# Retention attention and SwiGLU on one core: a hand-written opening order replaced by steps of the list scheduler

## The chip, the core and the metric

The kernel runs on one core of one Trainium2 chip. A core has a matrix engine (TensorE, PE; its weight loads are shown apart as PEld), three engines for elementwise work (VectorE, DVE; ScalarE, ACT; GpSimd, POOL), and a synchronisation engine (SP) that here issues the loads. Each engine works off its own queue in order; semaphores hold an instruction until what it needs is done. The metric is the device time of the run in microseconds (us).

## The reference

```python
def _attn_ref(q, k, v, lam):               # q, k, v: (4, 8, 768, 64) fp32
    ...
    for b in range(nb):                    # blocks of 64 positions
        intra = np.einsum('bhic,bhjc->bhij', qb, kb) * Dmask[None]
        intra = np.einsum('bhij,bhjd->bhid', intra, vb)
        inter = np.einsum('bhid,bhde->bhie', qb * lam_pow[None], kv_state)
        out[:, :, sl] = intra + inter
        kv_state = lam_block[None, :, None, None] * kv_state + np.einsum('bhsd,bhse->bhde', kb_dec, vb)

def _moe_ref(x, w_gate, w_val, w_out, rms_g):
    rms = np.sqrt(np.mean(x * x, axis=-1, keepdims=True) + 1e-06)
    xn = x / rms * rms_g
    g = xn @ w_gate                        # 512 -> 1536
    silu = g * (1.0 / (1.0 + np.exp(-g)))
    val = xn @ w_val
    return (silu * val @ w_out).astype(np.float32)
```

The output of the attention, 3072 tokens of 512 values, is the `x` of the second part.

## The kernel before, in words

The tokens are six groups `m` of 512. For each group the attention is done for four pairs `p` of heads (`Pair(m, p)`); then the rows are normed (`Norm`), and the group goes through the gated layer in twelve blocks `f` of 128 hidden columns (`Hidden(m, f)`). One such (m, f) is a unit `u`. Units 0 to 5 are group 0 with blocks 0 to 5, units 6 to 17 group 1 with all twelve, units 18 to 23 group 0 with blocks 6 to 11; group 0's rows are kept in `partial` in between. From unit 24 on come groups 2 to 5, in another form of the products (`tx`, `pa`, `pb`).

fp32 products are made of fp16 or f32r high and low parts, three products each (`hl`, `hh` against `wo`; high and low `x` against high and low `wg`, `wv`). For that, each weight block is loaded as integers (`raw_gv`, 1 MB; `raw_o`, 512 KB), lifted to floats by ACT (`lift`, L222), converted by DVE in two steps (`convert`, L231 and L234), squared by ACT for a norm (`square`, L446, output `junk`), summed over partitions on PE (`norm`, output `pn`, L451), scaled (`scale`, outputs `e`, `sc`), and split into a high part by ACT (L469) and a low part by DVE (L473). Later each block gets column sums of squares: ACT squares (`sq_w`, L305), DVE adds (`add`, L311; `last`, L314), and PE sums them (`pc`, L325), between the value matmuls of a unit.

The names of PE's outputs: `pa` scores, `pst` state sums, `po` mixes (attention out), `pss` row sums of squares, `pr` spread norms, `pg` gate, `pv` value, `acc` output product. DVE's `a` is a score tile times the decay mask (L533). `pc` and the second tile of `pa` share the PSUM bank `ps1`. `busy(n)` puts n matmuls of the identity with an unread output into PE's queue (`unread`), fillers in short. `load_next` issues the next load of a fixed list on SP's queue: the pairs `q1_0` to `q1_3` of group 1 between the weight blocks `gv1`, `gv2`, and so on; `load_o(f)` issues block f's output weights. A tile of tag `in` has four buffers, one of `raw_o` two: a load waits, and with it all that is queued behind it on SP, until the tile that had the buffer was read.

What sets the order: from unit 6 on a list scheduler (`Plan`) that knows for each step its engine, a cost in us, a due time `at` in units, the keys it reads (`r`) and writes (`w`) and the buffers it opens (`new`); it keeps a clock for each engine and emits the steps in order of their start. DVE steps in the set `SHARED` and POOL steps are taken to exclude each other. Units 0 to 5, the attention of groups 0 and 1, and weight blocks 0 to 5 are instead put in order by hand, by a function `ramp()` of some 360 lines, of which this is the beginning:

```python
        powers(2, 1)
        busy(4)
        powers(1, 2)
```

Of the kernel before, what the change touches and what calls it, by code (L numbers as in the profile page):

```python
# [9 lines left out]
F32 = mybir.dt.float32  # L10
# [13 lines left out]
def retention_swiglu_kernel(  # L24
# [67 lines left out]
    def load_gv(f):  # L92
        if f == 0:

            t = partial.bitcast(I32).rearrange("p a (b w) -> p (a b) w", w=2)
            t = t.rearrange("p (k o) w -> p k o w", k=2)
            for i in range(2):
                nc.sync.dma_start(t[:, i], w_all[f, :, i])
        else:
            t = stage.tile([P, 2, G, 2], I32, tag="in", name=f"raw_gv_{f}", bufs=4)  # L100
            nc.sync.dma_start(t, w_all[f, :, 0:2])
            if f <= 2:
                load_o(f - 1)
        raws[f] = t
# [37 lines left out]
    def busy(n, bank=2):  # L142

        ps = ps_out.tile([P, DM], F32, tag=f"po{bank}", name=f"unread{bank}")
        for _ in range(n):
            nc.tensor.matmul(ps[:, :P], ident, ident, start=True, stop=True)
# [37 lines left out]
    def scales():  # L184

        pmax = ps_out.tile([P, DM], F32, tag="po3", name="pmax")
# [209 lines left out]
    class Weights:  # L396
# [439 lines left out]
    def finish(m, f, hh, hl, half, ts=None):  # L836
        first = f == 0 or (m == 0 and f == HALF)
        last = f == NF - 1 or (m == 0 and f == HALF - 1)
        for t in ts or range(GC):
            out_product(m, f, hh, hl, t, first, last, m == 0, half)  # L840
            if last and m == 0 and f < HALF:
                out_rows(m, f, t, True, half)
# [210 lines left out]
    def ramp():  # L1053


        w0, w1, w2, w3, w4, w5, w6 = (Weights(f) for f in range(HALF + 1))
        h0, h1, h2, h3, h4, h5 = (Hidden(0, f) for f in range(HALF))
        p00, p01, p02, p03, p10, p11, p12, p13 = (Pair(m, p) for m in range(2) for p in range(NP))
        powers(0, 0)
        largest()  # L1060
        powers(0, 1)
        powers(2, 0)
        busy(2, 3)
        powers(2, 1)
        busy(4)
        powers(1, 2)
        powers(3, 1)
        powers(1, 0)
        powers(1, 1)
        p00.decay_k()  # L1070
        pm = scales()
        p00.scores()
        powers(0, 2)
        p00.decay_q(nc.gpsimd)
        busy(5)
        p00.decay_a()
        p00.state_sums()
        p01.decay_k()
        powers(3, 0)
        p01.scores()  # L1080
        p00.states()
        p01.decay_a()
        p00.mix_chunks()
        p01.state_sums()
        p01.decay_q(nc.gpsimd)
        p01.mix_chunks()
        p01.states()
        p02.scores()
        p00.mix_states()
        load_next()  # L1090
        powers(2, 2)
        p01.mix_states()
        load_next()
        powers(3, 2)
        p02.decay_k()
        p00.keep_squares()
        p00.keep_output(nc.scalar)
        p02.decay_a()
        p03.scores()
        scales_of(pm)  # L1100
        p03.decay_k()
        p01.keep_output(nc.scalar)
        row_sums(0, 0)
        p03.state_sums()
        p03.decay_q(nc.gpsimd)
        p02.decay_q(nc.gpsimd)
        p02.mix_chunks()
        p02.state_sums()
        p03.decay_a()
        p03.states()  # L1110
        p01.keep_squares()
        p03.mix_chunks()
        w0.lift()
        p02.states()
        p02.mix_states()
        load_next()
        p02.keep_squares()
        w0.convert(part=0)
        w0.convert(part=1)
        p03.mix_states()  # L1120
        load_next()
        p02.keep_output(nc.vector)
        row_sums(0, 1)
        p03.keep_squares()
        row_sums(0, 2)
        row_sums(0, 3)
        p03.keep_output(nc.scalar)
        w0.square(0)
        w0.square(1)
        w1.lift(0)  # L1130
        w1.lift(1)
        n0 = Norm(0)
        n0.mean()
        n0.root()
        p10.scores()
        p10.decay_a()
        busy(2, 3)
        w0.pn = w1.pn = ps_out.tile([P, DM], F32, tag="po3", name="pn_0")
        w0.norm()
        w1.convert(0)  # L1140
        p10.decay_k()
        w1.square(0)
        n0.spread()
        w0.scale()
        w1.convert(1)
        load_next()
        w0.high(0)
        w1.square(1)
        n0.scaled(0)
        n0.high(0)  # L1150
        p10.state_sums()
        busy(2, 1)
        w1.pn = w0.pn[:, 2:]
        w1.norm(slice(0, 1))
        w1.scale(slice(0, 1))
        n0.scaled(1)
        w0.high(1)
        n0.high(1)
        p10.states()
        n0.scaled(2)  # L1160
        n0.high(2)
        p10.mix_chunks()
        n0.scaled(3)
        busy(2, 3)
        n0.low(1, nc.vector)
        w0.low(0)
        n0.low(2, nc.vector)
        n0.high(3)
        n0.low(3, nc.vector)
        w0.lift_o()  # L1170
        w1.high(0)
        w0.low(1)
        w0.undo()
        w1.low(0)
        busy(2, 3)
        w1.pn = ps_att.tile([P, G], F32, tag="ps1", name="pn_1")
        w1.norm(slice(1, 2))
        w1.scale(slice(1, 2))
        p10.decay_q(nc.gpsimd)
        p10.mix_states()  # L1180
        load_next()
        p10.keep_output(nc.scalar)
        h0.gate(0)
        h0.val(0)
        h0.gate(1)
        n0.low(0, nc.gpsimd)
        h0.gate(2)
        h0.val(1)
        h0.val(2)
        w2.lift()  # L1190
        h0.silu()
        w2.convert(part=0)
        h1.gate(0)
        w1.undo()
        h0.mul()
        h1.gate(1)
        w3.lift()
        w1.high(1)
        h1.gate(2)
        w2.convert(part=1)  # L1200
        load_next()
        w1.low(1)
        w2.square(0)
        w2.square(1)
        h1.val(0)
        h1.val(1)
        w3.convert(part=0)
        w0.convert_o()
        p10.keep_squares()
        h1.silu()  # L1210
        w2.pn = ps_att.tile([P, G], F32, tag="ps1", name="pn_2")
        w2.norm()
        w2.scale()
        w2.high(0)
        p11.decay_k()
        w2.high(1)
        h1.val(2)
        p11.scores()
        h2.gate(0)
        w3.convert(part=1)  # L1220
        load_next()
        w2.low(0)
        high_o(0)
        w2.undo()
        h1.mul()
        h2.gate(1)
        w1.lift_o()
        w2.low(1)
        h2.gate(2)
        h2.val(0)  # L1230
        h2.val(1)
        h2.val(2)
        w3.square(0)
        h0.high()
        w1.convert_o()
        h0.low()
        low_o(0, nc.vector)
        h0.out(3)
        p11.decay_a()
        high_o(1)  # L1240
        h2.silu()
        h2.mul()
        w3.square(1)
        p12.decay_k()
        h0.out(2)
        p11.decay_q(nc.vector)
        w3.pn = ps_att.tile([P, G], F32, tag="ps1", name="pn_3")
        w3.norm()
        w3.scale()
        w2.lift_o()  # L1250
        h1.high()
        p11.state_sums()
        p11.states()
        w2.convert_o()
        w3.high(1)
        w3.high(0)
        p11.mix_chunks()
        w4.lift()
        w3.low(0)
        w3.low(1)  # L1260
        p12.scores()
        p11.mix_states()
        load_next()
        h3.gate(0)
        high_o(2)
        w3.undo()
        w4.convert(part=0)
        h3.gate(1)
        h0.out(0)
        h1.low()  # L1270
        h3.gate(2)
        p12.decay_q(nc.vector)
        w4.convert(part=1)
        load_next()
        p11.keep_squares()
        p11.keep_output(nc.scalar)
        low_o(1, nc.gpsimd)
        h3.val(0)
        h1.out(2)
        h3.val(1)  # L1280
        p12.decay_a()
        w3.lift_o()
        h3.val(2)
        h3.silu()
        h0.out(1)
        w4.square(0)
        w4.square(1)
        w4.pn = ps_att.tile([P, G], F32, tag="ps1", name="pn_4")
        w4.norm()
        p11.add_squares(nc.vector)  # L1290
        h3.mul()
        w4.scale()
        p12.state_sums()
        p12.states()
        p12.mix_chunks()
        p12.mix_states()
        load_next()
        w4.high(1)
        w4.high(0)
        w4.lift_o()  # L1300
        low_o(2, nc.vector)
        w4.low(1)
        w4.low(0)
        p12.keep_output(nc.vector)
# [709 lines left out]
```

## Time and profile before

| | |
|---|---|
| three runs | 661.6, 664.45, 664.99 us; median 664.45 |
| the profiled execution | 662.1 us, of which its span 660.3 |
| granted TensorE clock | 0.999 of full speed |
| HBM read, written | 44.05 MB, 6.29 MB |
| DMA packets | 14313, 51.13 MB |

The page gives for each engine its busy time, share of the span and number of instructions. In rows of instructions the columns are start and duration in us, engine, line, operation, output and inputs, shape, count (xN), and in brackets the idle time ahead of it and what ended it. A matmul's duration contains a tail that overlaps with the next one; the distance of two starts is what one adds. A fp32 matmul (`f32`) leaves two records.

### The profile page before, as it was taken

The numbers are of one execution on the slowest core, as the hardware profiler recorded it, in microseconds if no ns is written. First come the engines' busy times: TensorE is split into PE (matmuls) and PEld (weight loads), VectorE is DVE, ScalarE is ACT, GpSimd is POOL, SyncE is SP. The second block draws the span as 40 slices with busy tenths as digits, with TensorE's granted clock in tenths as the row PEclk, the third lists the DMA queues.
The fourth block names the chain that finished last, engine by engine and source line by source line (L and its number), as shares of the span: only waits on it lengthen the run. The fifth ranks groups of instructions, "written<-read, shape, count | busy, mean of one in ns | idle before, by whom it ended". The sixth has DMA issues, their size and how long they took to land.

```text
span 660.3 us, 12361 instructions
## 1 busy us (share of the span) xinstructions
PE 648.2 (98%) x5035; PEld 442.1 (67%) x5035; DVE 430.4 (65%) x826; ACT 333.5 (50%) x672; POOL 152.9 (23%) x132
## 2 busy tenths in 40 slices
PE   8999999999989999999999999999999999999997
PEld 8846664555555555777777777777777777777774
DVE  6798868889898867665474444488443488434333
ACT  3686648677754543454363434435444335433332
POOL 2300150003565845576110011003010102000000
PEclk9999999999999999999999999999999999999999
DMA  8976615331003200311100321100230000000001
GB/s 324 353 239 210 229 55 202 132 110 65 0 5 118 71 2 1 128 65 65 66 1 1 101 91 65 65 1 1 65 129 1 1 1 1 33 33 1 1 1 64
DMA packets 14313, 51.13 MB, mean 77 GB/s; under 512 B 1712, under 2 KB 1968, under 8 KB 12848
## 3 DMA queue, kind: packets, MB, share of 16 engines
q1 hardware_dynamic: 13968, 49.69, 21.3%
q8 instruction: 39, 0.64, 0.4%
q10 hardware_dynamic: 288, 0.66, 0.3%
q14 instruction: 18, 0.15, 0.1%
HBM read 44.05 MB, written 6.29 MB: 76 GB/s over the span
## 4 chain that ended last, share of the span: by engine, by line
PE 91%; DVE 5%; ACT 2%; issue 1%; DMA 1%; POOL 0%; DVEq 0%; POOLq 0%
PE pa L944 19%; PE pb L944 14%; PE acc L786 10%; PE acc L788 9%; PE acc L787 9%; PE pg L767 8%; PE pv L767 8%; PE pa L513 4%; PE po L578 3%; PE po L589 3%; PE pst L546 2%; PE pss L634 1%; DMA qkv<-in_qkv_dram 1%; ACT sq_w L305 1%; DVE sq_w L311 0%
## 5 line engine op out<-in xcount | busy, mean ns | idle before, releaser
L992 ACT COPY tx<-pa 128x256 f32<-128x256 f32 x144 | 53.6, 372 | 133.8 <-PE pa L944 133.0
L788 PE MATMUL acc<-wo,hh 128*128 128x512 f16 (+1 forms) x288 | 110.4, 383 | 0.0
L787 PE MATMUL acc<-wo,hh 128*128 128x512 f16 (+1 forms) x288 | 110.2, 383 | 0.0
L996 DVE TENSOR_TENSOR tx<-pb,tx 128x256 f32<-128x256 f32 x96 | 40.8, 425 | 71.2 <-PE pb L944 64.7
L786 PE MATMUL acc<-wo,hh 128*128 128x512 f16 x216 | 82.3, 381 | 0.2 <-DVE hh L1041 0.2
L944 PEld LDWEIGHTS <-wo 128*128 128x128 f16 x576 | 55.9, 98 | 26.9 <-issue 1.4
L1000 DVE TENSOR_TENSOR sg<-pb,tx 128x256 f32<-128x256 f32 x48 | 20.3, 424 | 77.7 <-ACT tx L992 77.7
L767 PE MATMUL pg<-x,wg 128*128 128x512 f16 x288 | 67.8, 380 | 1.7 <-ACT sg L1016 1.5
L767 PE MATMUL pv<-x,wv 128*128 128x512 f16 x288 | 67.4, 379 | 0.0
L944 PEld LDWEIGHTS <-wg 128*128 128x128 f16 x576 | 56.4, 98 | 16.1
L1034 ACT CAST hh<-sg 128x512 f16<-128x512 f32 (+1 forms) x72 | 44.5, 618 | 35.5 <-DVE sg L1010 16.7
L944 PEld LDWEIGHTS <-wv 128*128 128x128 f16 x576 | 56.4, 98 | 6.9
L537 POOL TENSOR_TENSOR qkv<-qkv,pw 128x512 f32<-128x512 f32 x22 | 29.1, 1323 | 102.5 <-PE pa L513 76.6
L767 PEld LDWEIGHTS <-wv 128*128 128x128 f16 x288 | 27.5, 98 | 35.7 <-issue 3.8
L767 PEld LDWEIGHTS <-wg 128*128 128x128 f16 x288 | 26.3, 98 | 36.4 <-issue 7.6
L1041 DVE TENSOR_TENSOR hh<-sg,hh 128x512 f16<-128x512 f32 x54 | 41.5, 769 | 3.4 <-ACT hh L1034 0.8
L1010 DVE SCALAR_TENSOR_TENSOR sg<-tx,cv,sg 128x512 f32<-128x512 f32 x48 | 39.2, 818 | 5.0
L944 PE MATMUL pb<-tx,wo 128*128 128x256 f16 x288 | 39.3, 273 | 0.6 <-DVE tx L996 0.6
L944 PE MATMUL pa<-tx,wo 128*128 128x256 f16 x288 | 39.3, 273 | 0.0
L944 PE MATMUL pa<-x,wv 128*128 128x256 f16 x288 | 39.3, 273 | 0.0
L944 PE MATMUL pb<-x,wv 128*128 128x256 f16 x288 | 39.3, 273 | 0.0
L944 PE MATMUL pb<-x,wg 128*128 128x256 f16 x288 | 39.3, 273 | 0.0
(183 smaller groups left out, 1160.9 us busy)
## 6 DMA issues: line engine op xcount, KB each, us to landing
qkv<-in_qkv_dram SPq DMA_DIRECT2D x47, 512.0 KB, 4.8
raw_gv<-in_weights_dram SPq DMA_DIRECT2D x11, 1024.0 KB, 5.4
raw_o<-in_weights_dram SPq DMA_DIRECT2D x12, 512.0 KB, 4.7
out_dram<-o SPq DMA_DIRECT2D x23, 256.0 KB, 2.1
partial<-in_weights_dram SPq DMA_DIRECT2D x2, 512.0 KB, 11.4
qkv<-in_qkv_dram ACTq DMA_DIRECT2D x1, 512.0 KB, 4.4
out_dram<-o SPq DMA_DIRECT2D x1, 128.0 KB, 1.7
out_dram<-o ACTq DMA_DIRECT2D x1, 128.0 KB, 2.4
```

What stands on the lines that cost most here:

```text
L513: nc.tensor.matmul(self.pa[j][:, c, :], self.kT[r, c, :], self.qT[r, c, :], start=True, stop=True,)
L537: eng.tensor_mul(self.qT, self.qT, pw[:, p : p + 1, :].broadcast_to([P, GC, P]))
L767: nc.tensor.matmul(ps, w[:, kk, :], x[:, kk, :], start=i == kk == 0, stop=i == 2 and kk == NK - 1,)
L786: nc.tensor.matmul(acc, hl[:, ts_], oh, start=first, stop=False)
L787: nc.tensor.matmul(acc, hh[:, ts_], ol, start=False, stop=False)
L788: nc.tensor.matmul(acc, hh[:, ts_], oh, start=False, stop=last)
L944: nc.tensor.matmul(ps, w(ow, k), x(ox, k), start=first and i == k == 0, stop=i == 2 and k == 1, skip_group_check=True,)
L992: nc.scalar.copy(self.kept[:, i], self.pa)
L996: nc.vector.tensor_add(self.val[:, half], self.pb, self.kept[:, i])
L1010: nc.vector.scalar_tensor_tensor(self.sg, self.val, cv[:, self.f : self.f + 1], self.sg, ALU.mult, ALU.mult)
L1034: nc.scalar.copy(self.hh, self.sg)
L1041: nc.vector.tensor_sub(self.hl, self.sg, hh)
```

## The change

`ramp()` is removed, and everything it did is given to the scheduler as steps: the arrival of the first loads, the mask powers, the attention of groups 0 and 1, the first norms, weight blocks 0 to 6, and units 0 to 5. With that come
- finer operand waits: in units 0 to 5 a gate or value product reads only the part of weights and activations it uses (`:h`, `:l`), and the rows of `partial` are four keys;
- `add`, `last`, `row_scales` and `powers` join the set `SHARED`;
- `load_o` is a step on the same queue of loads, right behind the next weight block, and not a call from the conversion of another block;
- the fillers come from the plan: where PE's next step starts more than 0.8 us after its last one ends, until the first `acc` opens;
- a table `SHIFTS` moves the due times of some 200 steps by an index into the list of steps.

```diff
         def convert_o(self, part=None):
             convert(self.bits, self.raw_o, part)
-            if part != 0 and self.f < HALF:
-                load_o(self.f + 2)
...
-    def ramp():
...
-        powers(2, 1)
-        busy(4)
-        powers(1, 2)
...
         SHARED = {
             "low", "low_o", "mul_sums", "sums", "refine", "rest_high", "convert", "convert_o",
-            "add_squares", "scale", "undo", "scaled_to",
+            "add_squares", "scale", "undo", "scaled_to", "row_scales", "last", "add", "powers",
         }
...
+            if u < HALF:
+                r = [f"w{name[1]}{f}:{'hlh'[i]}", *x_parts(m, o="hhl"[i])]
...
+        first_norm_steps(0, -0.3, 0.05)
+        for p, at in enumerate((-0.85, 1.05, 1.95, 3.05)):
+            q = Pair(1, p)
+            pair_scores(q, at)
+            pair_sums(q, at + 0.5)
+            pair_mix(q, at + 0.6)
...
+        def out_weights(f):
+            step("LD", 1.4, -9, load_o, f, w=[f"ro{f}"], new=[(f"ro{f}", "raw_o")], lasts=1.8)
...
+            step("LD", 2.8, -9, load_next, w=w, new=[(name, "in")], lasts=1.8)
+            if not p:
+                out_weights(m - 1)
...
+    SHIFTS = {
+        56: 1.6, 82: 1.1, 93: 1.5, 112: 2.05, 114: 0.25, 116: 0.3, 131: -2.4, 137: -17.9,
...
+        for i, by in SHIFTS.items():
+            eng, cost, at, *rest = plan.steps[i]
+            plan.steps[i] = (eng, cost, at + by, *rest)
         order = plan.run()
-        for _, i in order:
-            _, _, _, fn, args, *_ = plan.steps[i]
+        now, spare_bank = 1.5, True
+        for t, i in order:
+            eng, cost, _, fn, args, _, _, new, _ = plan.steps[i]
+            if eng == "PE":
+                if any(name.startswith("acc") for name, _ in new):
+                    spare_bank = False
+                idle = t - now
+                if spare_bank and idle > 0.8:
+                    busy(int((idle - 0.3) / 0.24))
+                now = t + cost
             fn(*args)
```

The fillers before are 2 and 4 ahead of the first scores, 5 behind them, and 2, 2, 2 and 2 ahead of the first gate, 19 in all; now they are 13 ahead of the first scores, 4 behind them, and 3 and 6 ahead of the first gate, 26. PE's real products are the same. Of PE's rows the last 5259 are in the same order. Three places where the order changes:

PE's queue around the norm of weight block 6, from the end of the values of unit 6 (`pv_0`) to the gate of unit 7 (`pg_1`). Before:

```order
L767 LDWEIGHTS wv
L767 MATMUL pv_0_1168<-x_530,wv 128x512
L451 LDWEIGHTS ones_b
L451 MATMUL pn_1185<-ssq_1145,ones_b 128x2
L767 LDWEIGHTS wg
L767 MATMUL pg_1_1190<-x_530,wg 128x512
```

After:

```order
L763 LDWEIGHTS wg
L763 MATMUL pg_1_1190<-x_524,wg 128x512
L447 LDWEIGHTS ones_b
L447 MATMUL pn_1215<-ssq_977,ones_b 128x2
L763 LDWEIGHTS wv
L763 MATMUL pv_1_1220<-x_524,wv 128x512
```

`pn` moved from ahead of the gate of unit 7 to behind it.

PE's queue at unit 16 (`pv_10`), where the column sums `pc` of two blocks stand between value matmuls. Ahead of these rows stand the scores `pa` of the first pair of group 2, before directly, after with eight gate matmuls between. Before:

```order
L786 MATMUL acc_0_1_1252<-wo_1510,hl_9_1905 128x512
L787 MATMUL acc_0_1_1252<-wo_1510,hh_9_1899 128x512
L788 MATMUL acc_0_1_1252<-wo_1510,hh_9_1899 128x512
L786 MATMUL acc_0_2_1259<-wo_1510,hl_9_1905 128x512
L787 MATMUL acc_0_2_1259<-wo_1510,hh_9_1899 128x512
L788 MATMUL acc_0_2_1259<-wo_1510,hh_9_1899 128x512
L767 LDWEIGHTS wv
L767 MATMUL pv_10_1935<-x_530,wv 128x512
L325 LDWEIGHTS sq_w_1815
L325 MATMUL pc<-ones_b,sq_w_1815 128x1
```

After:

```order
L782 MATMUL acc_0_3_1333<-wo_1253,hl_7_1740 128x512
L783 MATMUL acc_0_3_1333<-wo_1253,hh_7_1734 128x512
L784 MATMUL acc_0_3_1333<-wo_1253,hh_7_1734 128x512
L782 MATMUL acc_0_0_1310<-wo_1152,hl_6_1687 128x512
L783 MATMUL acc_0_0_1310<-wo_1152,hh_6_1680 128x512
L784 MATMUL acc_0_0_1310<-wo_1152,hh_6_1680 128x512
L782 MATMUL acc_0_0_1310<-wo_1253,hl_7_1740 128x512
L783 MATMUL acc_0_0_1310<-wo_1253,hh_7_1734 128x512
L784 MATMUL acc_0_0_1310<-wo_1253,hh_7_1734 128x512
L763 LDWEIGHTS wv
L763 MATMUL pv_10_1873<-x_524,wv 128x512
L323 LDWEIGHTS sq_w_1757
```

The eight gate matmuls and one more triple of `acc` now lie between the scores and `pc`, and the products are those of earlier units. On DVE the two `a` of these scores moved from behind the adds of the second block's `sq_w` to ahead of them.

SP's queue from the loads behind weight block 3 on (`qkv_2`, `qkv_3` are the pairs q1_2 and q1_3; the first `raw_gv` is block 4, the first `raw_o` block 2's output weights). Before:

```order
L86 DMA qkv_2_527<-in_qkv_dram 128x1024 x2
L101 DMA raw_gv_585<-in_weights_dram 128x2048
L109 DMA raw_o_605<-in_weights_dram 128x1024
L86 DMA qkv_3_641<-in_qkv_dram 128x1024 x2
L109 DMA raw_o_681<-in_weights_dram 128x1024
L109 DMA raw_o_728<-in_weights_dram 128x1024
L101 DMA raw_gv_761<-in_weights_dram 128x2048
```

After:

```order
L107 DMA raw_o_715<-in_weights_dram 128x1024
L86 DMA qkv_2_731<-in_qkv_dram 128x1024 x2
L101 DMA raw_gv_759<-in_weights_dram 128x2048
L107 DMA raw_o_782<-in_weights_dram 128x1024
L86 DMA qkv_3_800<-in_qkv_dram 128x1024 x2
L101 DMA raw_gv_833<-in_weights_dram 128x2048
L107 DMA raw_o_857<-in_weights_dram 128x1024
```

The output weights of block 2 moved ahead of q1_2, and from there on weight blocks, output weights and pairs take turns.

More of the change, by code (lines that the diff above doesn't have):

```diff
@@ L1603, in split_steps, with halved_steps, norm @@
-        step("DVE", 0.45, at + 0.8, wt.undo, r=[f"sc{f}"], w=[f"cg{f}"])
+            step("ACT", 0.72, at + 0.6 + 0.2 * i, wt.high, i, r=[f"wb{f}", f"sc{f}"], w=[w, w + ":h"])
+            step("DVE", 0.75, at + 0.7 + 0.2 * i, wt.low, i, r=[f"wb{f}", f"sc{f}"], w=[w, w + ":l"])
+        step("DVE", 0.45, at + 0.8, wt.undo, r=[f"sc{f}", "gs"], w=[f"cg{f}"])
+    def halved_steps(wt, at, i):
+        f = wt.f
+        c = slice(i, i + 1)
+        b = f"wb{f}_{i}"
+        def norm():
+            wt.pn = ps_att.tile([P, G], F32, tag="ps1", name=f"pn_{f}_{i}")
+            wt.norm(c)
+        new = [] if i else [(f"wb{f}_{j}", "o") for j in range(2)]
+        step("ACT", 0.66, at, wt.lift, i, r=[f"gv{f}"], w=[b], new=new)
+        step("DVE", 1.05, at + 0.1, wt.convert, i, r=[f"gv{f}"], w=[b])
+        step("ACT", 0.82, at + 0.2, wt.square, i, r=[b], w=[f"ssq{f}"],
+             new=[] if i else [(f"ssq{f}", "ssq")])
+        step("PE", 0.2, at + 0.3, norm, r=[f"ssq{f}"], w=[f"pn{f}_{i}"], new=[(f"pn{f}_{i}", "ps1")])
+        step("DVE", 0.35, at + 0.3, wt.scale, c, r=[f"pn{f}_{i}"], w=[f"sc{f}"],
+             new=[] if i else [(f"sc{f}", "sc")])
+        w = f"w{'gv'[i]}{f}"
+        step("ACT", 0.72, at + 0.4, wt.high, i, r=[b, f"sc{f}"], w=[w, w + ":h"])
+        step("DVE", 0.75, at + 0.45, wt.low, i, r=[b, f"sc{f}"], w=[w, w + ":l"])
+        if i:
+            step("DVE", 0.45, at + 0.5, wt.undo, r=[f"sc{f}", "gs"], w=[f"cg{f}"])
@@ L1638, in sum_steps @@
         places = (
-            [f"w16_{f}:s"], [f"third{f}"] + ["partial"] * (f >= HALF), [f"wg{f}"]
+            [f"w16_{f}:s"], [f"third{f}"] + [f"partial:{t}" for t in range(GC)] * (f >= HALF), [f"wg{f}"]
         )
@@ L1682, in out_steps @@
         weights = f"w16_{f}:o" if h.half else f"wo_{f}"
+        acc = f"acc{m}{'b' * (m == 0 and f >= HALF)}"
         for t, at in enumerate(ats):
             r = [f"hh{u}", weights] + ([] if h.half else [f"hl{u}"])
-            step("PE", 0.65 if h.half else 0.7, at, h.out, t, r=r, w=[f"acc{m}_{t}"],
-                 new=[(f"acc{m}_{t}", f"po{t}")] if first else [])
+            step("PE", 0.65 if h.half else 0.7, at, h.out, t, r=r, w=[f"{acc}_{t}"],
+                 new=[(f"{acc}_{t}", f"po{t}")] if first else [])
+            if m == 0 and f == HALF - 1:
+                step("ACT" if t % 2 else "DVE", 0.65, at - 0.5, out_rows, m, f, t, True, False,
+                     r=[f"{acc}_{t}"], w=[f"partial:{t}", "gv0"])
             if f < NF - 1:
@@ L1725, in pair_mix @@
              new=[(f"s{n}", "t" if p else "sq")])
-        if p:
+        if m == 0:
+            step("PE", 1.09, at + 0.3, row_sums, 0, p, r=[f"s{n}"], w=["pss0"], new=[] if p else [("pss0", "po2")])
+        elif p:
             eng = nc.vector if p == NP - 1 else nc.gpsimd
-            step("DVE" if p == NP - 1 else "POOL", 0.8 if p == NP - 1 else 1.3, at + 0.1, q.add_squares, eng,
+            step("DVE" if p == NP - 1 else "POOL", 0.7 if p == NP - 1 else 1.27, at + 0.1, q.add_squares, eng,
@@ L1729, in pair_mix, with first_norm_steps, mean, n @@
                  r=[f"s{n}"], w=[f"s{m}_0"])
+    def first_norm_steps(m, at, d):
+        norm = []
+        def mean():
+            norm.append(Norm(m))
+            norm[0].mean()
+        def n(name, *args):
+            def call():
+                getattr(norm[0], name)(*args)
+            call.__name__ = name
+            return call
+        if m:
+            step("PE", 0.95, at, row_sums, 1, 0, r=[f"s{m}_0"], w=[f"pss{m}"], new=[(f"pss{m}", "ps1")])
+        step("DVE", 0.2, at - 1, mean, r=[f"pss{m}"], w=[f"y{m}"])
+        step("POOL", 1.03, at - 1, n("root"), w=[f"y{m}"])
+        step("PE", 1.1, at, n("spread"), r=[f"y{m}"], w=[f"pr{m}"], new=[(f"pr{m}", "ps1" if m else "po2")])
+        for i, k in enumerate(range(NK)):
+            x = f"xn{m}_{k}"
+            step("DVE", 0.75, at - 1 + d * i, n("scaled", k), r=[f"x{m}:h{k}", f"x{m}:l{k}", f"pr{m}", "gs"], w=[x],
+                 new=[(x, "hl" if m == 0 and k > 1 else "t")])
+            step("ACT", 0.62, at - 1 + d * i + 0.05, n("high", k), r=[x], w=[f"x{m}:h{k}"])
+            low_at = at - 1 + d * i + 0.1
+            if k in LOW_POOL[m]:
+                step("POOL", 1.15, low_at, n("low", k, nc.gpsimd), r=[x, f"x{m}:h{k}"], w=[f"x{m}:l{k}"])
+            else:
+                step("DVE", 0.69, low_at, n("low", k), r=[x, f"x{m}:h{k}"], w=[f"x{m}:l{k}"])
```

477 lines of the change are left out of this document (86 added, 391 removed), and 22 rows, old and new, of the table SHIFTS.

## The prediction

> **What bounds the kernel now.** I read the engine totals first, then the chain that ended last, then the list of what TensorE (PE) waited for, and last the table by stretches of time.
>
> The totals and the chain from the page of before:
>
> ```profile
> PE 648.2 (98%) x5035; PEld 442.1 (67%) x5035; DVE 430.4 (65%) x826; ACT 333.5 (50%) x672; POOL 152.9 (23%) x132
> ...
> PE 91%; DVE 5%; ACT 2%; issue 1%; DMA 1%; POOL 0%; DVEq 0%; POOLq 0%
> ```
>
> PE is busy for 648.2 of 660.3 us and carries 91% of the chain. The change keeps PE's real products, so it can only win what PE does not spend on products: waits, and filler matmuls. The four largest rows of what PE waited for (line, releaser, then us in all, times, longest):
>
> ```profile
> PE pc L325 <- DVE a L533: 2.2, 1, 2.2
> PE unread L146 <- POOL power L135: 1.5, 1, 1.5
> PE pg L767 <- ACT sg L1016: 1.5, 1, 1.5
> PE pn L451 <- ACT junk L446: 1.1, 2, 0.8
> ```
>
> They come to 6.3 us, under 1%. The first 1.5 us is the making of the identity, ahead of everything. So 2.2 us at `pc`, 1.5 + 0.8 us around `pn` of weight block 6, and well under 1 us before the first gate remain. The table by stretches (window, its length, then busy us of PE, PEld, DVE, ACT, POOL, the clock, DMA share, GB/s):
>
> ```profile
> 20.00:30.00 10.00, 9.55 (x114) 8.32 (x112) 7.31 (x16) 6.69 (x15) 2.28 (x2) 1.00 0.99 394
> 30.00:40.00 10.00, 9.61 (x59) 4.90 (x56) 9.74 (x24) 8.30 (x14) 1.16 (x1) 1.00 0.68 229
> 50.00:60.00 10.00, 10.00 (x88) 6.53 (x87) 9.68 (x21) 7.74 (x15) 0.12 (x1) 1.00 0.62 222
> 90.00:100.00 10.00, 8.62 (x40) 4.75 (x39) 8.34 (x11) 4.67 (x11) 5.85 (x5) 1.00 0.12 29
> 180.00:200.00 20.00, 17.83 (x132) 11.00 (x130) 18.53 (x34) 10.88 (x21) 13.51 (x13) 1.00 0.11 32
> ```
>
> Three things to see. From 20 to 30 us the DMA engines are busy at 0.99: the loads set when the first weights arrive. From 30 to 40 and from 50 to 60 us PE has 9.6 and 10 of 10 and DVE 9.7: a new order there has almost nothing to win on PE and little room on DVE. In the stretches around 99 and 184 us PE has holes while DVE has 8.3 of 10 and 18.5 of 20: DVE was doing something else first.
>
> **The end does not move.** The last 5259 of PE's some 7200 rows stand in the same order before and after; the change ends at about unit 25. The later groups and the drain are kept.
>
> **The weight block 6 hole: minus 2.2 us.** Here PE's queue holds `pn` (norms of block 6) between the values of unit 6 and the gate of unit 7. The rows around it, of DVE, ACT and PE:
>
> ```profile
> 96.43 1.23 DVE L234 SCALAR_TENSOR_TENSOR w<-raw_gv,w 128x1024 int32<-128x1024 int32 x1
> ...
> 97.69 0.63 ACT L446 ACTIVATE junk<-w 128x512 bf16<-128x512 f32 x1 [4.37 <-DVE w L234]
> ...
> 99.22 0.16 PE L451 MATMUL pn<-ssq,ones_b 128*128 128x2 bf16 x1 [0.76 <-ACT junk L446]
> 100.83 2.75 PE L767 MATMUL pg<-x,wg 128*128 128x512 f16 x12 [1.45 <-ACT sg L1016]
> ...
> 100.11 0.67 ACT L1016 ACTIVATE sg<-pg,cg 128x512 f32<-128x512 f32 x1
> ```
>
> DVE converts block 6 until 97.66, ACT squares it until 99.2, PE waits 0.76 us with `pn` at the head of its queue, and then 1.45 us because ACT's silu (which frees the gate bank) stood behind the squares. 0.76 + 1.45 = 2.21. In the new order the gate of unit 7 stands ahead of `pn`, and the products of unit 5 are spread among the gates of units 6 and 7, so that ACT has its silu out earlier. Both waits lose their cause. Nothing queued behind the moved `pn` is needed sooner than before: block 6's scales go to unit 12's stage. Bounds: 1.45 (only the second wait goes) to 2.2; I take 2.2, since the row of the gate is what the wait list names.
>
> **The column norm hole: minus 2.0 us.** The sums `pc` use the PSUM bank of the second score tile; so `pc` waits for DVE's second `a` (L533), which reads that tile. DVE and PE there:
>
> ```profile
> 180.41 1.24 DVE L311 TENSOR_TENSOR sq_w<-sq_w 128x512 bf16<-128x512 bf16 x1 [2.72 <-ACT sq_w L305]
> 181.68 1.27 DVE L314 TENSOR_TENSOR sq_w<-sq_w 128x256 bf16<-128x256 bf16 x1
> 182.87 0.68 DVE L533 TENSOR_TENSOR a<-pa,mask 128x512 f32<-128x512 f32 x1
> 183.47 0.91 DVE L311 TENSOR_TENSOR sq_w<-sq_w 128x512 bf16<-128x512 bf16 x1
> 184.30 0.68 DVE L533 TENSOR_TENSOR a<-pa,mask 128x512 f32<-128x512 f32 x1
> ...
> 185.40 0.28 DVE L314 TENSOR_TENSOR sq_w<-sq_w 128x256 bf16<-128x256 bf16 x1
> ...
> 179.62 0.71 PE L513 MATMUL pa<-qkv 64*128 64x128 f32 x8
> 181.07 0.39 PE L786 MATMUL acc<-wo,hl 128*128 128x512 f32 x1
> 182.47 0.39 PE L767 MATMUL pv<-x,wv 128*128 128x512 f16 x1
> 185.03 0.16 PE L325 MATMUL pc<-ones_b,sq_w 128*128 128x1 bf16 x1 [2.17 <-DVE a L533]
> ```
>
> The scores end at 180.3, but the two `a` start at 182.87 and 184.30, behind adds that wait 2.72 us for ACT's squares and then run long beside POOL (1.27 us for a form that takes 0.28 at 185.40). PE's cover from scores to `pc` is three triples of output products and one value matmul, 2.4 us. In the new order both `a` come ahead of the adds, and PE's cover is eight gate matmuls (8 x 0.216, since twelve in the row at 100.83 take 2.75 us with the last one's tail of 0.38), four triples (4 x 0.71, from 181.07 to 182.47 for two) and one value matmul: 1.7 + 2.8 + 0.2 = 4.8 us, against 1.3 us of `a`. The late adds now meet PE at the third `pc`, 0.4 us on: two `a`, four small sums and the adds, 1.3 + 1.6 (an estimate: four at 0.4, between the 0.28 and the 0.68 of the fence) + 0.7 to 2.5 us is 3.6 to 5.4 us against 5.2. So 2.2 us goes and 0 to 0.2 us comes back; bounds 1.0 (ACT's squares late by another 1 us) and 2.2, taken 2.0.
>
> **The start: plus 0.3 us.** PE's first rows:
>
> ```profile
> 1.47 2.93 PE L146 MATMUL unread<-ident 128*128 128x128 f32 x12 [1.47 <-POOL power L135]
> 5.16 2.08 PE L513 MATMUL pa<-qkv 64*128 64x128 f32 x16 [0.24 <-DMA qkv<-in_qkv_dram]
> 7.17 1.38 PE L146 MATMUL unread<-ident 128*128 128x128 f32 x10
> 8.49 0.69 PE L546 MATMUL pst<-qkv 128*64 128x64 f32 x16
> ```
>
> A filler leaves two records. The twelve cold ones take 2.93 us with the last one's tail (0.58), which spaces them at 0.213 and makes 0.427 us a filler; the ten later ones take 1.38 with a tail of 0.38, 0.223 us a filler. The first scores take 2.08 us, 1.1 would be the warm time by the same ratio. The clock therefore rises between about 6.8 and 7.4 us. The new order has 13 fillers ahead of the scores: at the cold price they end at 1.47 + 13 x 0.427 = 7.02, while the data is there at 5.16; the scores then run mostly warm and end at 8.1 to 9.1, and four fillers (0.9) follow: `pst` at 9.0 to 10.0 instead of 8.49, 0.5 to 1.5 us late. If the clock rises as early as it can after the fillers began, all is 0.5 us early. Most of a loss is swallowed before the first gate:
>
> ```profile
> 24.55 1.23 ACT L222 ACTIVATE w<-raw_gv 128x512 f32<-128x512 f32 x2 [0.30 <-DMA raw_gv<-in_weights_dram]
> ...
> 30.37 1.48 PE L146 MATMUL unread<-ident 128*128 128x128 f32 x8
> 33.82 0.38 PE L767 MATMUL pg<-x,wg 128*128 128x512 f16 x1 [0.28 <-ACT x L725]
> ```
>
> PE idles or runs fillers there (eight from 25 us on, the last four in the row at 30.37; the new order has nine), because the gate waits for ACT and DVE, which wait for the load of weight block 1 at 24.55. SP's queue is unchanged to block 3, so this arrival stays. By adding the rows of the new order one after the other I get the fourth gate matmul at 33.7 to 34.4, now 33.82. Taken +0.3, bounds -0.5 and +1.0.
>
> The Trainium skill, "TensorE: Matmul & The Clock Gate", section "Part 1: The HAM clock gate (the "warmup" mystery)", says that the rise comes after a busy window of 3413 ns that runs freely and does not start with the kernel. By that rule the fillers' end is anywhere from 6.0 to 7.0 us, and the sum would be 657.7 to 659.5 where my cold price gives 658.5; the trace agrees in so far as the rise lies some 5.6 us, more than one such window, after the first matmul.
>
> **Behind the first gate: plus 0.3 us.** DVE now makes two low activations ahead of the gate weights' low half of block 0; PE reaches these about 0.3 us early by the same adding up. Bounds 0 and 0.7. The other finer waits and the earlier output rows are priced at nothing: between 35 and 98 us PE is full before, and DVE and ACT do the same work in all.
>
> **The SP queue: nothing, with a sharp edge.** The new queue has the output weights of block 2 ahead of the pair q1_2 (before: two of SP's issues, the conversion that frees a buffer, the high and low half of unit 1's hidden values, and the landing time of such a load):
>
> ```profile
> 40.57 0.33 SPq L101 DMA_DIRECT2D raw_gv<-in_weights_dram  x1
> 42.86 0.33 SPq L109 DMA_DIRECT2D raw_o<-in_weights_dram  x1
> ...
> 42.14 0.69 DVE L234 SCALAR_TENSOR_TENSOR wg<-raw_o,wg 128x512 int32<-128x512 int32 x1
> 56.03 0.69 DVE L1041 TENSOR_TENSOR hl<-sg,hh 128x512 fp32r<-128x512 f32 x1
> ...
> 50.89 0.60 ACT L1034 CAST hh<-sg 128x512 fp32r<-128x512 f32 x1
> ...
> raw_o<-in_weights_dram SPq DMA_DIRECT2D x12, 512.0 KB, 4.7
> ```
>
> That load waits until block 0's output weights are converted (before: 42.83). The conversion is now 20 rows later on DVE; ahead of it came two `a` (1.3), a step of block 3's conversion (1.2), three low halves of weights and two steps of hidden values (at about 0.7 each, 3.5) and small ones (1): some 6.5 us when they overlap by 0.1 each, so the issue is at about 49.5. With 4.7 us to landing, and then 1 MB at 394 GB/s, q1_2 is there at about 57; its scores stand at about 58 on PE. Block 4 and the rest queue behind. Slack 1 to 1.5 us: cost 0, and 1 us of PE for each us beyond.
>
> **Sum.** The profiled execution took 662.1 us: 662.1 - 2.2 - 2.0 + 0.3 + 0.3 = 658.5. It lies 2.35 us under the median of 664.45; scaled, 658.5 x 664.45 / 662.1 = **660.8 us**, 0.55% less.
>
> **Rivals.**
> - *Given back.* DVE at 9.7 of 10 from 30 to 60 has no room, and a list scheduler with fixed costs doesn't see POOL's stretching. The freed 4.2 us come back as small waits in 35 to 180 us. For it: DVE idles some 2 us for the late load above and then lags. Against: PE had 8.62 of 10 at 90 to 100 and DVE only that hole. Time: 662.1 + 0.6 - (0 to 2) = 660.7 to 662.7, so 663 to 665.
> - *The queue, slower.* `hl` of unit 1 now stands ahead of the conversion of block 0's output weights on DVE; before it ran only at 56.03. If its input (ACT's high half, at 50.89 before) stays as late as it was, the conversion ends at about 55.3, the load of block 2 lands at 60, q1_2 at 62.7: PE idles 4.7 us at q1_2's scores, and block 4's 2.6 us of load behind it cost some 2.3 more. From an issue at 51 on it costs; at 55.3 it is 658.5 + 7 = 665.5, so 668.
> - *More is won.* Fillers and waits from 25.6 to 33.8 sum to 4 us, the five early fillers to 1.1: with the first gate 2 us earlier, 656.5, so 658.8. All of it gone would be 653.5. Against: the load at 24.55.
> - *It does not do what it says* (no wait is moved): 662.1, or 664.5; part of the first rival.
>
> **Chances.** A measurement of this kernel tells about 0.5%, 3.3 us, from no change. Forecast 0.45, given back 0.26, more won 0.16, queue 0.13. The forecast's bounds put 0.27 of its 0.45 below 661.1; with 0.16 and a little of the second, faster is 0.45; same 0.42; slower 0.13. The range 657.0 to 666.5 leaves out the deep end of the won case and most of the queue case; the forecast's own range, with all bounds together, is 659.5 to 663.7.
>
> **What would show it.** Right: no wait at `pn` and gate near 99 us or at `pc` near 184; `pst` after 9 us; the fourth gate matmul at 33.7 to 34.4; SP's issue of block 2's output weights at 48 to 51 and no DMA wait of scores. Wrong: a wait of PE over 1 us between 35 and 98, a DMA named as releaser of `pa`, or a first gate before 33.

## The result, and the profile after

| | before | after |
|---|---|---|
| median of 11 runs | 663.34 us (661.6 to 666.85) | 659.80 us (659.3 to 660.05) |
| ratio | | 0.994, 95% interval 0.9924 to 0.9957 |
| the profiled execution, its span | 662.1, 660.3 us | 659.59, 657.8 us |
| granted TensorE clock of the profiled execution | 0.999 | 1.0 |

The changed kernel is 0.6% faster by the ratio of the runs (the medians alone differ by 0.53%); the interval does not reach 1. Two things stand in this table beside the ratio: the profiled executions differ by 2.5 us, the medians by 3.5; and the runs of before spread over 5 us, those of after over less than 1.

The page of after, the totals and the chain, and the list of TensorE's (PE's) waits:

```profile
PE 650.3 (99%) x5049; PEld 442.4 (67%) x5049; DVE 425.0 (65%) x823; ACT 335.5 (51%) x674; POOL 151.3 (23%) x133
...
PE 96%; DVE 2%; ACT 1%; issue 0%; POOL 0%; DVEq 0%; POOLq 0%
...
PE unread L144 <- POOL ident masks.py:199: 1.5, 1, 1.5
PE acc L782 <- DVE hh L1035: 0.7, 2, 0.5
PE pb L938 <- DVE tx L990: 0.6, 1, 0.6
PE pn L447 <- DVE a L529: 0.3, 1, 0.3
```

The rows `pc <- DVE a` (2.2), `pg <- ACT sg` (1.5) and `pn <- ACT junk` (1.1) are gone. Output products that wait for VectorE's (DVE's) low part of hidden values had 0.2 us in before's list (`PE acc L786 <- DVE hh L1041: 0.2, 1, 0.2`) and have 0.7 now: a wait of 0.5 us is new. The table by stretches, three rows of before and then those of after (window, its length, busy us of PE, PEld, DVE, ACT, POOL, the clock, DMA share, GB/s):

```profile
34.00:100.00 66.00, 64.62 (x426) 39.32 (x425) 56.07 (x106) 42.91 (x81) 12.70 (x10) 1.00 0.53 181
100.00:120.00 20.00, 19.17 (x88) 10.41 (x88) 17.71 (x37) 16.34 (x31) 0.00 (x0) 1.00 0.62 223
200.00:270.00 70.00, 69.97 (x501) 39.65 (x500) 53.82 (x89) 32.41 (x62) 40.75 (x34) 1.00 0.17 59
...
25.00:34.00 9.00, 8.72 (x87) 7.23 (x88) 8.15 (x22) 8.71 (x19) 3.46 (x3) 1.00 0.94 350
34.00:100.00 66.00, 65.98 (x425) 38.16 (x424) 58.74 (x107) 47.89 (x88) 16.22 (x12) 1.00 0.54 204
100.00:120.00 20.00, 19.96 (x93) 11.24 (x92) 17.41 (x35) 14.62 (x28) 0.00 (x0) 1.00 0.32 108
180.00:200.00 20.00, 20.00 (x126) 12.35 (x125) 16.47 (x31) 9.62 (x18) 14.89 (x14) 1.00 0.16 53
200.00:270.00 70.00, 69.44 (x528) 40.67 (x527) 49.91 (x84) 33.48 (x63) 40.64 (x34) 1.00 0.13 46
```

From 34 to 200 us PE has no hole of 0.1 us left; 34 to 100 had 64.62 of 66 busy, 100 to 120 had 19.17 of 20, 180 to 200 had 17.83. The one new hole, 0.5 us, lies in the last row. From 274 us to the end each product of after starts 2.50 us ahead of the same one of before: nothing moves there.

The two places in PE's timeline of after, block 6's norm and the column sums:

```profile
98.18 1.90 PE L763 MATMUL pg<-x,wg 128*128 128x512 f16 x8
99.91 1.03 PE L763 MATMUL pv<-x,wv 128*128 128x512 f16 x4
100.78 1.03 PE L763 MATMUL pg<-x,wg 128*128 128x512 f16 x4
101.64 0.17 PE L447 MATMUL pn<-ssq,ones_b 128*128 128x2 bf16 x1
101.85 2.75 PE L763 MATMUL pv<-x,wv 128*128 128x512 f16 x12
...
177.01 0.39 PE L763 MATMUL pv<-x,wv 128*128 128x512 f16 x1
177.24 0.17 PE L323 MATMUL pc<-ones_b,sq_w 128*128 128x1 bf16 x1
177.26 0.38 PE L763 MATMUL pv<-x,wv 128*128 128x512 f16 x1
177.48 0.17 PE L323 MATMUL pc<-ones_b,sq_w 128*128 128x1 bf16 x1
```

No bracket stands behind `pn` or `pc`: neither waits. The start, and the way into the first gate:

```profile
1.47 4.96 PE L144 MATMUL unread<-ident 128*128 128x128 f32 x26 [1.47 <-POOL ident masks.py:199]
6.36 1.16 PE L509 MATMUL pa<-qkv 64*128 64x128 f32 x16
7.45 1.16 PE L144 MATMUL unread<-ident 128*128 128x128 f32 x8
8.54 0.69 PE L542 MATMUL pst<-qkv 128*64 128x64 f32 x16
...
31.62 1.60 PE L144 MATMUL unread<-ident 128*128 128x128 f32 x12
33.18 0.18 PE L447 MATMUL pn<-ssq,ones_b 128*128 128x1 bf16 x1
33.22 1.13 PE L763 MATMUL pg<-x,wg 128*128 128x512 f16 x4
```

The 26 records of fillers take 4.96 us, between the all-cold 26 x 0.213 = 5.5 and the warm 2.9: the clock rose while they ran (the records' spacing turns from 0.213 to 0.112 us at 5.26), and the scores take 1.16 us, not 2.08.

### The profile page after: what moved, and what is told of

Its sections match the earlier page's. It is cut to its first block, busy times and chain, and to the rows that moved or that the text cites. A ratio compares the mean times of both kernels' runs of the same rounds, so it can differ in the third digit from the quotient of the medians.

```text
span 657.8 us, 12390 instructions
## 1 busy us (share of the span) xinstructions
PE 650.3 (99%) x5049; PEld 442.4 (67%) x5049; DVE 425.0 (65%) x823; ACT 335.5 (51%) x674; POOL 151.3 (23%) x133
## 4 chain that ended last, share of the span: by engine, by line
PE 96%; DVE 2%; ACT 1%; issue 0%; POOL 0%; DVEq 0%; POOLq 0%
PE pa L938 19%; PE pb L938 14%; PE acc L782 10%; PE pv L763 10%; PE pg L763 9%; PE acc L784 9%; PE acc L783 9%; PE pa L509 4%; PE po L574 4%; PE po L585 3%; PE pst L542 2%; PE unread L144 1%; PE pss L630 1%; DVE hh L1035 1%; PE pr L663 0%; DVE sg L1004 0%
## 5 line engine op out<-in xcount | busy, mean ns | idle before, releaser
L763 PE MATMUL pv<-x,wv 128*128 128x512 f16 x288 | 69.5, 379 | 0.0
L533 POOL TENSOR_TENSOR qkv<-qkv,pw 128x512 f32<-128x512 f32 x24 | 31.3, 1303 | 101.9 <-PE pa L509 67.5
L938 PE MATMUL pa<-x,wg 128*128 128x256 f16 x288 | 39.3, 273 | 0.0
```

Source lines behind the costliest of these rows:

```text
L533: eng.tensor_mul(self.qT, self.qT, pw[:, p : p + 1, :].broadcast_to([P, GC, P]))
L763: nc.tensor.matmul(ps, w[:, kk, :], x[:, kk, :], start=i == kk == 0, stop=i == 2 and kk == NK - 1,)
L938: nc.tensor.matmul(ps, w(ow, k), x(ox, k), start=first and i == k == 0, stop=i == 2 and k == 1, skip_group_check=True,)
```

## The experiments

Theories before the first runs: A, the spread of before comes from the start, where the clock rises early or late; B and C, the two waits have the causes that the prediction named, and each can be taken away in the kernel before by itself; the rival in each case is that the win comes back elsewhere. Each kernel was timed beside the kernel before on the same chip.

**1. The long start in the kernel before.** 13 fillers ahead of the first scores.

```diff
-        busy(4)
+        busy(11)
```

> The kernel before with 13 instead of 6 filler matmuls ahead of the first scores. Theory A (before's runs spread from 661.6 to 666.9 us because the clock of TensorE rises late in some of them, while after's 13 fillers in one piece bring it up early each time): the runs lie within 1.5 us of each other, at 661.0 to 662.5, median 1.0 to 2.0 us under that of before. Rival (the spread has another source, and the start is worth nothing): the spread stays at 4 us or more and the median moves by less than 0.5 us.

Measured: 664.49 us (663.7 to 666.85), 1.0024 of before (1.0009 to 1.0039). Theory A falls: the runs still spread over 3.2 us and the median rises by 0.9. Its rival, which gave the start less than 0.5 us, misses too: the fillers cost time, since in the profile the clock rises only at 7.0 us, as they end, and PE's products from the first state sums to the first hole come 1.3 us later than in the profile of before. This profile, at 666.5 us and a granted clock of 0.993, also shows where the spread is from. PE's rows behind the two holes, and two stretches with their granted clock (the number behind POOL's):

```profile
100.51 0.16 PE L451 MATMUL pn<-ssq,ones_b 128*128 128x2 bf16 x1 [0.75 <-ACT junk L446]
102.12 4.44 PE L767 MATMUL pg<-x,wg 128*128 128x512 f16 x12 [1.45 <-ACT sg L1016]
106.40 2.75 PE L767 MATMUL pv<-x,wv 128*128 128x512 f16 x12
...
188.00 0.16 PE L325 MATMUL pc<-ones_b,sq_w 128*128 128x1 bf16 x1 [2.17 <-DVE a L533]
188.02 0.59 PE L767 MATMUL pv<-x,wv 128*128 128x512 f16 x1
...
190.81 2.37 PE L767 MATMUL pg<-x,wg 128*128 128x512 f16 x9
...
102.59:105.99 3.40, 3.40 (x10) 1.16 (x9) 2.67 (x9) 3.40 (x7) 0.00 (x0) 0.50 0.57 214
187.92:191.33 3.41, 3.33 (x12) 1.61 (x12) 2.62 (x9) 1.53 (x3) 0.14 (x1) 0.50 0.02 5
```

Twelve gate matmuls take 4.44 us here, 2.75 in the profile of before; a value matmul takes 0.59 us behind `pc`, 0.38 in other rows. Behind each hole the granted clock is 0.50 for 3.4 us. That is theory D: a hole of 2.2 us costs its own length and, in part of the runs, some 1.6 us of slow clock behind it. It sorts the runs of before by their granted clock (55 timed beside the experiments): 12 at 0.999, median 661.5 us; 21 at about 0.996, median 663.4; 22 at about 0.993, median 664.5.

**2. The short start in the changed kernel.** 6 fillers instead of 13.

```diff
-        now, spare_bank = 1.5, True
+        now, spare_bank, most = 1.5, True, 6
...
-                    busy(int((idle - 0.3) / 0.24))
+                    busy(min(most, int((idle - 0.3) / 0.24)))
+                    most = 99
```

> The changed kernel with 6 instead of 13 fillers ahead of the first scores, all else as it is. Theory A: some runs are 1.5 to 5 us longer than the fastest, median 660.3 to 662, and the profile shows the first scores at the slow spacing. Rival: 659.3 to 660.1 in every run, as with 13.

Measured: 658.49 us (658.12 to 660.79); four runs at 658.1 to 658.5, two at 660.8. Theory A is right that some runs are 2.3 us longer and that the scores are slow in them, but its median, 660.3 or more, is missed, and so is the rival's single level. The start makes levels too, though not those of before: the profile of a 660.8 run has scores of 2.08 us and then four fillers of 2.07. With 13 fillers the median is about 1.3 us higher, and none of the eleven runs of the result shows a second level.

**3. The seam told to the scheduler.** In the kernel before, VectorE is free 4.5 us after the scheduler's zero (as the trace shows: unit 6 begins at 93.1, the conversion of block 6 ends at 97.7).

```diff
             clock = dict.fromkeys(self.ENGINES, 0.0)
+            clock["DVE"] = 4.5
...
+                if fn == w6.square:
+                    from_deps[i] = 4.5
```

> The kernel before; the scheduler is told the state at its seam with the hand-written part: VectorE free only 4.5 us after it begins, weight block 6 converted only then. On TensorE the only row that moves is the norm sum of block 6, to behind the gate of unit 7. Theory B (the scheduler took VectorE for idle at the seam, so put that norm too early): the two waits of 0.8 and 1.5 us near 99 us go, the time falls by 2.2 us (1.8 to 2.4) and stays won to the end. Rival (given back): the wait list names another wait of 1 us or more between 95 and 180 us and the time falls by less than 1 us.

Measured: 659.80 us (658.95 to 660.37), 0.9945 (0.9927 to 0.9963). These few lines of state give as much as the whole change. Against before, its profiled products start 0.78 us earlier ahead of the hole and 3.30 us earlier behind it: 2.5 us, and no wait in its place. Behind the other hole, which is still there, this execution loses 1.6 us again:

```profile
181.72 0.16 PE L325 MATMUL pc<-ones_b,sq_w 128*128 128x1 bf16 x1 [2.17 <-DVE a L533]
...
183.26 4.43 PE L767 MATMUL pg<-x,wg 128*128 128x512 f16 x12
```

Theory B holds. Its median falls by 3.75 us against before's beside it, more than the 2.2 expected; the likely reason is that one of the two falls of the clock went too.

**4. The mask products ahead of the adds.** In the kernel before, two VectorE rows move up by two and three places.

```diff
         order = plan.run()
+        late = [j for j in range(first - 24, second) if named[j][1].__name__ in ("add", "last")]
...
+            *(o for j, o in enumerate(order[: second + 1]) if j not in late), *moved, *order[second + 1 :],
```

> The kernel before; the two mask products of the first pair of group 2 stand ahead of the adds of column squares on VectorE, nothing else moves. Theory C (the column sums waited for the bank that these mask products free, and they stood behind adds waiting for ScalarE): the 2.2 us wait near 183 us goes; a wait of 0 to 1.2 us for the adds is left, since the cover on TensorE is as short as before: 1.0 to 2.2 us less. Rival (VectorE is full there, whatever its order): 0 to 0.7 us less, the wait stays over 1.5 us.

Measured: 662.24 us (660.78 to 662.53), 0.9977 (0.9965 to 0.999). The wait of 2.2 us is gone, and two smaller ones stand for it:

```profile
PE pg L767 <- DVE state L561: 0.4, 1, 0.4
PE pc L325 <- DVE sq_w L314: 0.4, 1, 0.4
```

In the profile 0.8 us is won at this place, less than the 1.0 to 2.2 expected (the medians differ by 1.3 us, but hold falls of the clock): theory C names the cause rightly, but moving the two rows alone gives two thirds of it back, for the adds and state updates behind them are now late. The changed kernel has no wait there; it also laid 2.4 us more of PE's work ahead of `pc`, which no run tried by itself.

**5. The holes filled, not closed.** In the kernel before, nine unread matmuls run in the first hole, and ten matmuls that add zeros to an output bank in the second.

```diff
+            fill = 3 * (self.f == HALF)
+            for _ in range(fill):
+                nc.tensor.matmul(self.pn[:, 3 * P :], ident, ident, start=True, stop=True)
             self.norm()
...
+                for _ in range(10):
+                    nc.tensor.matmul(accs[0][:, :P], zero, ident, start=False, stop=False)
```

> The kernel before; both holes stay in the order, but are filled with unread matmuls: 3 ahead of and 6 behind the norm sum of block 6 near 99 us, and 10 (adding zeros to an open output bank) ahead of the column sums near 183 us. Theory D (each hole of 2.2 us lets the clock of TensorE fall to half for some 3 us behind it in part of the runs; 0, 1 or 2 such falls make the three levels of before at 661.4, 663.2 and 664.5 us): every run has a clock of 0.998 or more and lies within 1 us of 661.5; the median falls by 1.5 to 2.3 us though no wait is removed. Rival (the levels come from the start or the loads): the runs stay spread over 3 us, median within 0.7 us of before.

Measured: 661.44 us (661.14 to 661.99), 0.997 (0.9953 to 0.9987); the clock is 0.999 or 1.0 in all twelve runs. PE's rows where the second hole was:

```profile
182.34 2.39 PE L328 MATMUL acc<-ident,zero 128*128 128x128 f32 x20
184.68 0.16 PE L331 MATMUL pc<-ones_b,sq_w 128*128 128x1 bf16 x1
...
186.22 2.12 PE L778 MATMUL pg<-x,wg 128*128 128x512 f16 x9
```

`pc` comes no earlier behind the value matmul ahead of it (2.56 us here and before), but the upper two levels are gone. This settles theory D: an idle array, not the loads or the start, made before's levels, and of its median some 2 us were slow clock.

**6. Without the table of shifts.**

```diff
-        for i, by in SHIFTS.items():
+        for i, by in ():
```

> The changed kernel without the table of shifts: the list scheduler with the due times as they are written. Theory E (the table makes the order; the scheduler alone plans idle time on TensorE ahead of the first gate and in the first units): 4 to 10 us slower than the changed kernel, slower than before by 0.2 to 0.9%, with new waits of 1 us or more on TensorE between 30 and 180 us. Rival (the steps and the seam alone carry the win): within 1 us of 659.8.

Measured: 665.84 us (665.09 to 666.92), 1.004 (1.0026 to 1.0054). Theory E holds: 6 us slower than with the table. The time is not lost in new waits of 1 us, as expected, but mostly ahead of the first gate:

```profile
31.75 3.84 PE L144 MATMUL unread<-ident 128*128 128x128 f32 x32
36.03 0.18 PE L447 MATMUL pn<-ssq,ones_b 128*128 128x1 bf16 x1 [0.45 <-DVE e L454]
36.99 1.04 PE L763 MATMUL pg<-x,wg 128*128 128x512 f16 x4 [0.78 <-ACT wg L465]
```

The first gate waits for ScalarE's (ACT's) weights, behind sixteen planned fillers and another wait, and comes at 36.99 instead of 33.22 us: 3.8 of the 6.7 us between the two profiles. The other 2.9 us come behind it, where the plan has seven more fillers between 46 and 52 us. The steps alone are slower than the hand-written order; the table makes the difference.

**7. Eight fillers at the start of the changed kernel.** As in experiment 2, with 8.

> The changed kernel with 8 instead of 13 fillers ahead of the first scores: they end at 4.9 us when cold, just as the first data lands. Theory F (what costs at the start is fillers that run past the landing; what costs in two of six runs with 6 fillers is the pause before it): 658.1 to 658.7 us in every run, 1.1 to 1.7 us under the changed kernel. Rival: two levels as with 6 fillers, 658.3 and 660.8, or no gain over 13 fillers since the first gate waits for ScalarE and VectorE.

Measured: 658.90 us (658.54 to 659.27), one level. 0.9 us won rather than 1.1 to 1.7. The pause ahead of the first data is the likely cause of the two levels of experiment 2; six runs against six can't prove it, but experiment 10, with the same eight fillers, has one level too. In the profile all comes 0.91 us earlier from the first state sums on, and it stays 0.91 to 0.94 to the end.

**8. Experiments 3 and 4 together in the kernel before.**

> The kernel before with the seam told to the scheduler and the two mask products ahead of the adds, that is both small repairs together; some 20 rows of the order differ from before. Theory D: 2.5 + 0.8 us off the fast level of before (661.4), and no fall of the clock, since no hole of 2 us is left: 657.9 to 658.6 us in every run, 0.8% under the median of before and 1 us under the changed kernel. Rival: the changed kernel's other edits carry part of its win, and this stays at or above 659.8 us.

Measured: 658.16 us (658.0 to 658.49), 0.9928 (0.9909 to 0.9946). The sum comes out as expected, and its median is 1.6 us under that of the changed kernel, with the hand-written opening left in place.

**9. The new wait near 207 us.** In the changed kernel two neighbouring VectorE rows are exchanged: the low part of unit 18's hidden values, step `j`, goes ahead of the output copy, step `k`.

```diff
+        k = max(n for n in range(j) if names[n][0] == "DVE")
...
+        order.insert(k, order.pop(j))
```

> The changed kernel with two neighbouring VectorE rows exchanged near 205 us: the low part of the hidden values of unit 18 ahead of the copy of an output tile of group 1. Theory G (the new wait of 0.5 us of an output product near 207 us is part of what the change gave back): that wait goes and the time falls by 0.4 to 0.6 us, to 659.2 to 659.4. Rival (the copy, now later, holds a bank that TensorE wants next): the wait moves on and the time stays within 0.2 us of 659.8.

Measured: 659.48 us (658.96 to 660.04). The wait list loses the 0.5, and between 194 and 207 us the profile gains 0.56 us on that of the changed kernel; in the runs it is 0.3 us, less than the 0.4 to 0.6 expected, with overlapping ranges.

**10. Experiments 7 and 9 together.**

> The changed kernel with 8 fillers at the start and the exchange of the run before: the two add up, 0.9 + 0.5 us, to 658.3 to 658.6 us with no run over 659. Rival: they overlap and it stays at 658.9.

Measured: 658.27 us (657.67 to 658.73): 0.6 us less than with the fillers alone and 1.2 less than with the exchange alone, so they add up.

**11. A third repair in the kernel before.** Beside experiment 8, the state updates stand ahead of the second pair of adds.

> The kernel before with the two repairs, and the state updates of the first pair of group 2 ahead of the second pair of adds, so that the gate's bank comes free earlier: the wait of 0.4 us of the gate near 182 us goes. 657.7 to 657.9 us, the fastest of all. Rival: the adds are then late for the next column sums and 0.3 us or more comes back: 658.1 or more.

Measured: 657.88 us (657.77 to 658.52), 0.9915 (0.9897 to 0.9934), the lowest median of all. The wait of the gate is gone, while one of 0.4 us of scores for `en` is new; 0.3 us on experiment 8 lies within both ranges.

**12. The pair ahead of the output weights on SP.** In the changed kernel q1_2 and weight block 4 are issued ahead of block 2's output weights again.

```diff
+        for n in (2, 1):
+            order.insert(loads[ro2][0], order.pop(loads[ro2 + n][0] + (n == 1)))
```

> The changed kernel with the pair q1_2 and weight block 4 again ahead of block 2's output weights on SP's queue. Theory H (the new order of the queue costs nothing, as priced): within 0.3 us of 659.8, with q1_2 issued some 15 us earlier. Rival (TensorE or ScalarE does lose time to the late loads, without a wait that the list shows): 0.5 us or more faster. The late load itself (block 2's output weights) now stands behind 2 MB more and may come later: 0 to 0.5 us slower by that.

Measured: 660.14 us (659.48 to 660.69). SP's issues in the changed kernel, and then here:

```profile
51.22 0.33 SPq L107 DMA_DIRECT2D raw_o<-in_weights_dram  x1
51.66 0.84 SPq L86 DMA_DIRECT2D qkv<-in_qkv_dram  x2
...
32.83 1.82 SPq L86 DMA_DIRECT2D qkv<-in_qkv_dram  x2
40.76 0.33 SPq L101 DMA_DIRECT2D raw_gv<-in_weights_dram  x1
52.22 3.43 SPq L107 DMA_DIRECT2D raw_o<-in_weights_dram  x2
```

The pair is issued 19 us earlier and nothing is won: theory H holds, though the median is 0.34 us up where 0.3 was allowed. In the profile all of the distance to the changed kernel, 1.05 us, is there at the first state sums (the clock rose at 7.56 us in this execution), and it is 1.07 at the end: the queue's order changed nothing.

## Why the prediction came out, and where its sum did not

**Block 6's norm, -2.2: right.** Both waits are gone in the changed kernel; experiment 3 gives 2.5 us for this alone. The cause was more general than "`pn` stands too early": the scheduler began with all engines idle at its zero, while VectorE had 4.5 us of the hand-written order before it.

**Column sums, -2.0: right.** No wait at 177 us; experiment 4 shows that the order on VectorE was the cause, and that this order alone, with PE's shorter cover, leaves 0.8 us of other waits.

**The start, +0.3: near, by luck.** The first state sums are at 8.54, not 9.0 to 10.0, because the clock rose at 5.26 us in this execution; the fourth gate matmul is at 33.22 + 3 x 0.216 = 33.87, in the predicted 33.7 to 34.4 and 0.05 us behind before's. The step that failed is the sentence that most of a loss is swallowed before the first gate, since the load of weight block 1 stays where it was. It does not stay: its issue comes at 16.09 us in the changed kernel, 17.15 in experiment 12 and 15.19 in experiment 7, by as much as the start is late or early. In experiment 12, whose opening is that of the changed kernel, the state sums are at 9.59 and the whole 1.05 us is still there at the first gate and at the end; the 1.3 us of experiment 1 reach the first gate whole, too. In experiment 12 the fourth gate matmul is 1.1 us behind before's, past the bound of 1.0, and fewer fillers save 0.9 us (experiment 7). One reading of the sum is off as well: the upper end of 657.7 to 659.5 adds 1.0 to the 0.3 that it already holds; in its place it gives 659.2.

**Behind the first gate, +0.3:** the third group of gate matmuls starts about 0.2 us late (0.39 us from the last value matmul at 34.84, where others take 0.22), and there is no wait to 98 us. Right within its bounds.

**The SP queue, 0: right, with a thinner edge than priced.** Experiment 12 shows that the order cost nothing. The load came at 51.22 us, where 48 to 51 was said and cost from 51 on; q1_2's first reader waited for it, and PE's scores followed 0.44 us later:

```profile
58.42 0.91 ACT L519 ACTIVATE qkv<-qkv,mask 128x256 f32<-128x256 f32 x2 [0.91 <-DMA qkv<-in_qkv_dram]
...
58.86 1.16 PE L509 MATMUL pa<-qkv 64*128 64x128 f32 x16
```

How much each us beyond the edge costs was not tried.

**The sum: -3.6 in the profiled execution, -2.5 measured.** The mis-sized step is the sentence that prices everything else behind the first gate at nothing. Of the 4.4 us of waits that left, 0.6 came back as new waits, 0.5 of them at 207 us; experiment 9 takes that one away and wins 0.56 us in its profile. About 1.2 us more came back without a wait: PE's same products, from the fourth gate matmul to 274 us, take that much longer. The changes from one kind of product to another rise there from 206 to 229, and by the spacings of the rows they cost some 0.6 to 0.9 us more in after (an estimate: what each change adds over going on with the same product). No run tested this alone; it stays open.

**The medians: -0.55% predicted, -0.60% measured (-0.53% by the medians).** That they agree is partly luck. The prediction scaled its sum to the median as if the distance of the profiled execution from it were noise. It was the slow clock behind the two holes: 0, 1 or 2 falls of 1.6 us. The order alone is worth 661.5 - 659.8 = 1.7 us between the runs of before without a fall and the median of after (the profiles say 2.5, but that of before lies 0.6 above those runs and that of after 0.2 under its median); the rest of the 3.5 us between the medians is clock that no longer falls. A mechanism that the prediction did not have thus made up for what its sum claimed too much.

**The rivals.** "Given back" was right by about 1.8 of 4.4 us; "queue" stayed 0.44 us from its edge; "more is won" did not happen, and experiment 7 shows that 0.9 us of it was there to be had at the start. Experiments 8 and 11 reach 658.2 and 657.9 us another way, with the hand-written opening kept.

## What to carry to other kernels

When a list scheduler takes over from an order made elsewhere, give it the state of every engine's queue at the seam: a few lines did as much here as the removal of the seam. A hole of some 2 us on the matrix engine cost here its length and, in part of the runs, 1.6 us of slow clock behind it, and a few unread matmuls in the hole bought that second part back. If runs of one kernel cluster, sort them by granted clock, and look in the profile of the slowest for a common row that takes longer than elsewhere.

## What was not expected of the hardware

A pause of 2.2 us, even one broken by a small norm sum after 0.8 us, was enough for the clock to fall: by the granted clock, in 43 of 55 runs of before at one or both of its places. The slow stretch lasted 3.41 us and cost some 1.6 us (twelve matmuls of 4.44 instead of 2.75 us); whether it comes changes from run to run, with the same program.

The traces hold a likely reason. In each of the profiles all changes of the granted clock lie whole multiples of 3.413 us apart: in experiment 1 the two falls come 28 and 53 of these behind the rise at 7.01 us, and each lasts one. In the three falls that were profiled (two in experiment 1, one in experiment 3), the interval of this grid ahead of the fall held 2.2, 2.1 and 1.9 us of idle PE. In the profile of before, without a fall, a line of the grid cuts the same pauses into 0.76 and 1.45 us, and into 1.82 and 0.35. So what differs between the runs seems to be where the pauses lie in the grid; no run moved a pause to test it.

The rise at the start varies likewise: at 5.26 us in the profile of after, at 5.99 and 7.56 in those of experiments 9 and 12 with the same opening, at 7.19 in that of before, and at 7.01 in experiment 1, whose 26 filler records all ran cold:

```profile
1.46 5.80 PE L146 MATMUL unread<-ident 128*128 128x128 f32 x26 [1.46 <-POOL power L135]
```
